# A Fourier mixer followed by a SoLU layer: an entry's first steps begin two steps later, output weights converted without ScalarE, five weight buffers, nine idle products ahead of the step back

## Chip, cores, metric

One core of a Trainium2 chip. The metric is the device time of one execution in microseconds (us), the median of several; lower is better.

## The reference

```python
# mixing: x (8, 3136, 256), filt_r / filt_i (1569, 256)
X = np.fft.rfft(x, axis=1)
Y = X * (filt_r + 1j * filt_i)[None]
y = np.fft.irfft(Y, n=3136, axis=1).astype(np.float32)
# SoLU layer on the 25088 rows of y: w_in (256, 1024), w_out (1024, 256), g_ln (1024)
h = y.reshape(-1, 256) @ w_in
s = h * softmax(h)
ln = (s - mean(s)) / sqrt(var(s) + 1e-6) * g_ln
out = ln @ w_out
```

The weights `w_in` and `w_out` come in 64 bits and are converted to 32 on the core.

## The kernel before

The eight batch entries go one by one through four kinds of work: **first steps** (a short Fourier matrix on rows of x), a **spectrum** (second Fourier step, filter, inverse), and **steps back** (matmuls with `wi_t`, line 353, giving rows of y). Entry 0 does all of this in an *opening* before the main loop. The main loop has 205 *steps* of one block of 128 tokens; each does the SoLU layer of a block and, between its matmuls, pieces of the later entries. `PLAN` says in which step each piece falls: first steps, spectrum units, steps back. "Third entry" is `PLAN[2]`.

```python
PLAN = [
    None,
    ([0, 0, 0, 0, 1, 1, 1, 1], [4, 5, 6, 7, 8, 10, 12], [16, 17, 18, 19, 20, 20, 21, 22]),
    (range(1, 17, 2), range(18, 32, 2), [34, 36, 38, 40, 42, 43, 44, 46]),
    ([17, 23, 25, 27, 29, 31, 33, 35], range(38, 52, 2), range(54, 70, 2)),
    # ... entries 4 to 7
```

Both first steps and steps back read a tile of rows, taken in turn from four buffers. The step in which a row tile is fetched follows from the plan:

```python
    row_loads.sort(key=lambda load: load[0])          # by the step t that uses it
    for n, (t, latest, earliest, load) in enumerate(row_loads):
        at = max(t - 3, earliest, min(row_loads[n - 4][0] + 1, latest) if n >= 4 else -1)
        if at < 0:
            load()
        else:
            loads[at].append(load)                     # issued at the end of step `at`
```

So a tile goes out three steps ahead if it can, but not before the step after the use of the tile four places earlier in the list (`latest` and `earliest` bound this). Loads for the steps back are issued by GpSimd, those of first steps from the third entry on by SyncE.

The end of the opening (`convert` turns one of eight weight pieces to 32 bits; `back` is one step back; its argument is the copy on ScalarE that takes the result out of PSUM; an idle product is a matmul whose result nobody reads, there to keep TensorE busy):

```python
        for i in range(units):
            # ... spectrum of entry 0
            elif i in (1, 3, 4):
                begin({1: 2, 3: 3, 4: 4}[i])           # fetch a weight piece
        idle_row(7, "idler")                           # seven idle products on TensorE
        # ... fetch the rows of the step back, of entry 1, store the filter table (SyncE)
        rest = {2: convert(2)}
        rest.pop(2)()
        begin(5)
        rest[3] = convert(3)
        for ch in range(pieces):
            if ch in (0, 2, 4, 6):
                j = 3 + ch // 2
                rest.pop(j)()                          # ScalarE and GpSimd part of weight j
                if j < 5:
                    begin(j + 3)
                rest[j + 1] = convert(j + 1)           # VectorE part of the next
                if j == 3:
                    weight_sums(w_in_sb)
            for cb in range(KD):
                back(0, ch, cb, nc.scalar.copy)
        rest.pop(7)()
```

## Time and profile before

| | before |
|---|---|
| median, range (first chip, 4 runs) | 1689.76 us, 1688.36 to 1693.68 |
| span of the profiled run, clock | 1694.6 us, 0.981 |
| TensorE busy | 94% |
| VectorE, GpSimd, ScalarE busy | 74%, 67%, 55% |

The clock is the mean share of full speed granted to TensorE; the text calls TensorE cold where it is 0.50 and warm where it is 1.00. The lines that carry the argument are in the prediction.

### The profile page before, as it was taken

How to read it: one execution, taken by the hardware profiler on the slowest of the kernel's cores; microseconds unless marked ns; L12 is line 12 of the kernel's file. 1: busy time of each engine (PE TensorE's matmuls, PEld its weight loads, DVE VectorE, ACT ScalarE, POOL GpSimd, SP SyncE). 2: the span in 40 equal slices, each digit the busy share in tenths (PEclk: the TensorE clock that was granted, in tenths of full speed). 3: DMA queues.
4: the chain of work that ended last, by engine and by line, in shares of the span. 5: the costliest groups of instructions: out<-in, count | busy, mean ns of one | idle time of the engine just before them, and what ended most of it. 6: DMA issues, size and time to landing. Idle time of an engine off the chain costs nothing.

```text
span 1694.6 us, 31047 instructions
## 1 busy us (share of the span) xinstructions
PE 1600.7 (94%) x10008; PEld 1098.7 (65%) x10008; DVE 1259.3 (74%) x2619; ACT 940.0 (55%) x1734; POOL 1131.5 (67%) x1272
## 2 busy tenths in 40 slices
PE   5786899999999999999999999999999999999996
PEld 1362356766766677667766676666776777777776
DVE  1684786788777878787778878787778767777772
ACT  2153456655655565566565665656555666655551
POOL 4463787568756866787568865688556766676664
PEclk8987999999999999999999999999999999999999
DMA  9884767887788768866787658766786455444443
GB/s 262 242 280 151 233 196 195 220 225 196 186 231 237 190 164 228 242 174 167 195 233 212 179 151 226 214 188 170 187 211 176 116 129 123 101 110 102 110 110 94
DMA packets 375957, 311.72 MB, mean 184 GB/s; under 512 B 61514, under 2 KB 341571, under 8 KB 375795
## 3 DMA queue, kind: packets, MB, share of 16 engines
q1 hardware_dynamic: 306260, 169.81, 38.6%
q0 software_dynamic: 32640, 101.65, 20.3%
q10 hardware_dynamic: 36896, 38.28, 8.0%
q8 instruction: 81, 1.33, 0.3%
q14 instruction: 80, 0.66, 0.1%
HBM read 124.83 MB, written 81.50 MB: 122 GB/s over the span
## 4 chain that ended last, share of the span: by engine, by line
PE 62%; DMA 18%; DVE 9%; SPq 3%; POOL 3%; issue 3%; ACT 2%; ACTq 0%; DVEq 0%; POOLq 0%
PE m L682 25%; PE o L794 25%; DMA solu_t<-turn 7%; PE py L353 5%; DMA out_dram<-ot 3%; DMA x<-in_x_dram 2%; SPq L752 2%; PE pa L260 2%; PE pb L292 2%; PE pc L292 2%; DVE h L730 2%; DVE turn L740 1%; DMA t<-d 1%; DVE diff L245 1%; DVE h L706 1%
## 5 line engine op out<-in xcount | busy, mean ns | idle before, releaser
L732 ACT ACTIVATE e<-h,nmu 128x1024 f32<-128x1024 f32 x196 | 225.3, 1150 | 363.4 <-DVE h L730 361.7
L794 PEld LDWEIGHTS o<-w_out_sb,solu_t 128*128 128x128 f32 x3136 | 381.0, 192 | 56.7 <-issue 39.7
L794 PE MATMUL o<-w_out_sb,solu_t 128*128 128x128 f32 x3136 | 401.4, 276 | 8.1 <-DVE rsum L725 4.9
L682 PE MATMUL m<-w_in_sb,s 128*128 128x512 f32 x784 | 400.8, 603 | 2.1 <-ACT h L692 1.9
L794 PEld LDWEIGHTS o<-w_out_sb,u 128*128 128x128 f32 x2352 | 305.6, 192 | 147.2 <-issue 111.6
L660 POOL TENSOR_TENSOR u<-solu_t 128x512 f32<-128x512 f32 x98 | 143.5, 1464 | 305.3 <-DMA solu_t<-turn 190.0
L682 PE MATMUL m<-w_in_sb,y 128*128 128x512 f32 x588 | 315.8, 621 | 25.2 <-DVE nmax L706 22.6
L794 PE MATMUL o<-w_out_sb,u 128*128 128x128 f32 x2352 | 313.2, 276 | 6.9 <-ACT ot L806 5.2
L730 DVE SCALAR_TENSOR_TENSOR h<-e,rsum,h 128x1024 f32<-128x1024 f32 x196 | 286.9, 1464 | 6.9
L813 DVE SCALAR_TENSOR_TENSOR ot<-o,rs_t,ot 128x128 f32<-128x128 f32 x294 | 102.6, 349 | 211.8 <-ACT ot L806 175.0
L692 ACT COPY h<-m 128x512 f32<-128x512 f32 x294 | 173.7, 591 | 127.3 <-PE m L682 117.7
L740 DVE STREAM_TRANSPOSE turn<-h 128x1024 f32<-128x1024 f32 x196 | 242.3, 1236 | 0.8
L714 ACT ACTIVATE e<-h,nmax 128x1024 f32<-128x1024 f32 x196 | 226.2, 1154 | 0.0
L660 POOL TENSOR_TENSOR u<-solu_t,u 128x512 f32<-128x512 f32 x98 | 143.1, 1460 | 87.5 <-PE o L794 83.3
L706 DVE CUSTOM_DVE_ANT_0 h<-m,h 128x512 f32<-128x512 f32 x196 | 133.2, 679 | 76.8 <-ACT h L692 51.3
L682 PEld LDWEIGHTS m<-w_in_sb,y 128*128 128x128 f32 x588 | 96.0, 193 | 134.4 <-DVE nmax L706 76.0
L353 PEld LDWEIGHTS py<-wi_t,t 100*128 100x128 f32 x1024 | 136.8, 198 | 57.2 <-issue 42.0
L356 ACT COPY y<-py 128x392 f32<-128x392 f32 x128 | 109.1, 854 | 103.3 <-PE py L353 101.8
L682 PEld LDWEIGHTS m<-w_in_sb,s 128*128 128x128 f32 x784 | 124.3, 191 | 62.8 <-issue 46.1
L660 POOL TENSOR_TENSOR solu_t<-solu_t,solu_t 128x512 f32<-128x512 f32 x98 | 152.6, 1557 | 7.7
L660 POOL TENSOR_TENSOR u<-u,solu_t 128x512 f32<-128x512 f32 x98 | 140.5, 1433 | 0.7
L353 PE MATMUL py<-wi_t,t 100*128 100x98 f32 x1024 | 136.0, 279 | 4.7 <-ACT y L356 3.5
(106 smaller groups left out, 1979.5 us busy)
## 6 DMA issues: line engine op xcount, KB each, us to landing
solu_t<-turn SPq DMA_DIRECT2D x784, 128.0 KB
out_dram<-ot SPq DMA_DIRECT2D x196, 128.0 KB
t<-d POOLq DMA_DIRECT2D x56, 400.0 KB, 5.0
d<-x POOLq DMA_DIRECT2D x100, 200.0 KB, 4.9
f<-f_dram POOLq DMA_DIRECT2D x39, 512.0 KB, 6.7
d<-g POOLq DMA_DIRECT2D x39, 512.0 KB, 5.0
t<-d ACTq DMA_DIRECT2D x36, 512.0 KB
x<-in_x_dram SPq DMA_DIRECT2D x112, 98.0 KB
```

The source lines that it names most:

```text
L353: nc.tensor.matmul(out=psv[:, i:2 * NCH - i:2 * NCH - 1 - 2 * i, :], lhsT=t4s[e, ch][:, i, cb * P:cb * P + P], rhs=wi_t, start=True, stop= ...
L356: evac(out=y[:, cb, t0:t0 + S].rearrange("p (r m j) -> p m j r", m=N2 // NCH, j=NCH)[:, ch:last + 1 - ch:last - 2 * ch], in_=psv.rearrange ...
L660: nc.gpsimd.tensor_tensor(out=out, in0=in0, in1=in1, op=op)
L682: nc.tensor.matmul(out=ms[j, bank], lhsT=lhsT, rhs=w_in_sb[:, w, :], start=m in (1, 2, 7), stop=True, skip_group_check=True)
L692: nc.scalar.copy(out=h_half(k, i), in_=ms[j, 0])
L706: nc.vector.tensor_tensor_reduce(out=h_half(k, i), in0=ms[j, bank], in1=h_half(*kept), scale=1.0, scalar=sofar, op0=ALU.add, op1=ALU.min, ...
L714: nc.scalar.activation(out=e, in_=hs[k], func=AFT.Exp, bias=nmaxs.pop(k)[:, 1:2], scale=-1.0, accum_out=esum)
L730: nc.vector.scalar_tensor_tensor(out=solu, in0=e, scalar=rsum, in1=solu, op0=ALU.mult, op1=ALU.mult, accum_out=nmu)
L732: nc.scalar.activation(out=e, in_=solu, func=AFT.Square, bias=nmu, scale=-float(DFF), accum_out=variances[g][:, i:i + 1])
L740: nc.vector.transpose(out=turns[g][:, :, i, :], in_=solus.pop(k).rearrange("p (f j) -> p f j", j=32))
L794: nc.tensor.matmul(out=pos[p, bank], lhsT=lhs[:, f, :], rhs=w[:, f, :], start=f == 0 and m in (1, 2, 7), stop=True, skip_group_check=True)
L813: nc.vector.scalar_tensor_tensor(out=ot, in0=pos[p, bank], scalar=rs, in1=out_half(p, *kept)[0], op0=ALU.mult, op1=ALU.add)
```

## The change

The intent is to start the third entry's first steps when their rows have arrived (step 3, not 1), and to free the step back of entry 0 from the weight conversions between which it was threaded.

```diff
-    (range(1, 17, 2), range(18, 32, 2), [34, 36, 38, 40, 42, 43, 44, 46]),
-    ([17, 23, 25, 27, 29, 31, 33, 35], range(38, 52, 2), range(54, 70, 2)),
+    (range(3, 19, 2), range(20, 34, 2), [36, 38, 39, 40, 42, 43, 44, 46]),
+    ([19, 23, 25, 27, 29, 31, 33, 35], range(38, 52, 2), range(54, 70, 2)),
...
-        wpool = pool("wp", 3, stack=st)
+        wpool = pool("wp", 5, stack=st)
... (load_float64, for the output weights)
+                ts(out=power, in0=power, scalar1=255.0, scalar2=2.0 ** 23, op0=ALU.min, op1=ALU.mult)
...
-            def finish():
-                nc.scalar.mul(rest, lo, 2.0 ** -44)
-                nc.gpsimd.tensor_tensor(out=rest, in0=rest, in1=power.bitcast(FP32), op=ALU.mult)
-                nc.gpsimd.tensor_tensor(out=dst, in0=dst, in1=rest, op=ALU.add)
+            if share:                                  # input weights: as before
+                nc.scalar.mul(rest, lo, 2.0 ** -44)
+                nc.gpsimd.tensor_tensor(out=rest, in0=rest, in1=power.bitcast(FP32), op=ALU.mult)
+            else:                                      # output weights: VectorE
+                stt(out=rest, in0=lo, scalar=2.0 ** -44, in1=power.bitcast(FP32), op0=ALU.mult,
+                    op1=ALU.mult)
+            nc.gpsimd.tensor_tensor(out=dst, in0=dst, in1=rest, op=ALU.add)
...
-            elif i in (1, 3, 4):
-                begin({1: 2, 3: 3, 4: 4}[i])
-        idle_row(7, "idler")
+            elif i != 2:
+                begin({1: 2, 3: 3, 4: 4, 5: 5, 6: 6}[i])
+        idle_row(9, "idler")
...
-        (conversions threaded through the step back, as shown above)
+        convert(2)
+        begin(7)
+        convert(3)
+        convert(4)
+        weight_sums(w_in_sb)
+        for j in (5, 6, 7):
+            convert(j)
+        for ch in range(pieces):
             for cb in range(KD):
                 back(0, ch, cb, nc.scalar.copy)
```

More of the change, by code (lines that the diff above doesn't have):

```diff
@@ L372, in load_words, with load_float64 @@
             return raw
-        def load_float64(dst, raw, negate=False):
+        def load_float64(dst, raw, negate, share):
             lo, hi = raw[:, :, 0], raw[:, :, 1]
@@ L385, in load_float64 @@
             ts(out=power, in0=power, scalar1=896.0, scalar2=0.0, op0=ALU.subtract, op1=ALU.max)
-            ts(out=power, in0=power, scalar1=255.0, scalar2=None, op0=ALU.min)
-            ts(out=power, in0=power, scalar1=23, scalar2=-2 ** 31 if negate else 0,
-               op0=ALU.logical_shift_left, op1=ALU.bitwise_or)
+            if negate:
+                ts(out=power, in0=power, scalar1=255.0, scalar2=None, op0=ALU.min)
+                ts(out=power, in0=power, scalar1=23, scalar2=-2 ** 31, op0=ALU.logical_shift_left,
+                   op1=ALU.bitwise_or)
+            else:
+                ts(out=power, in0=power, scalar1=255.0, scalar2=2.0 ** 23, op0=ALU.min, op1=ALU.mult)
             stt(out=power, in0=hi, scalar=-2 ** 31, in1=power, op0=ALU.bitwise_and,
@@ L393, in load_float64 @@
             nc.vector.tensor_tensor(out=frac, in0=frac, in1=power, op=ALU.bitwise_or)
-            def finish():
+            if share:
                 nc.scalar.mul(rest, lo, 2.0 ** -44)
                 nc.gpsimd.tensor_tensor(out=rest, in0=rest, in1=power.bitcast(FP32), op=ALU.mult)
-                nc.gpsimd.tensor_tensor(out=dst, in0=dst, in1=rest, op=ALU.add)
-            return finish
+            else:
+                stt(out=rest, in0=lo, scalar=2.0 ** -44, in1=power.bitcast(FP32), op0=ALU.mult,
+                    op1=ALU.mult)
+            nc.gpsimd.tensor_tensor(out=dst, in0=dst, in1=rest, op=ALU.add)
         filters, tables = {}, {}
@@ L496, in convert @@
         def convert(j):
-            return load_float64(weights[j][0], raws.pop(j), negate=j < 4)
+            load_float64(weights[j][0], raws.pop(j), negate=j < 4, share=j < 4)
         for j in range(2):
-            convert(j)()
+            convert(j)
         def start(i):
@@ L545 @@
                 in_=f[0:rows, at:at + n].rearrange("p i k c -> p i (k c)"))
-        rest = {2: convert(2)}
-        rest.pop(2)()
-        begin(5)
-        rest[3] = convert(3)
-        for ch in range(pieces):
-            if ch in (0, 2, 4, 6):
-                j = 3 + ch // 2
-                rest.pop(j)()
-                if j < 5:
-                    begin(j + 3)
-                rest[j + 1] = convert(j + 1)
-                if j == 3:
-                    weight_sums(w_in_sb)
+        convert(2)
[4 more added lines that the diff above has]
+        for j in (5, 6, 7):
+            convert(j)
+        for ch in range(pieces):
             for cb in range(KD):
                 back(0, ch, cb, nc.scalar.copy)
-        rest.pop(7)()
     ps_b = [pool(f"ps_b{u}", 1, PSUM) for u in range(2)]
```

## The prediction

> **What bounds the kernel now.** I read the page's slices first, then who waited for whom, stretch by stretch, then the engines in order of time. The tenths of busy time over 40 slices (42.4 us each):
>
> ```profile
> PE   5786899999999999999999999999999999999996
> PEclk8987999999999999999999999999999999999999
> ```
>
> TensorE fills its slices from the sixth on (about 212 us), so the steady steps are bound by its work, which the change does not alter. What can be won is idle or slow TensorE time in the first four or five slices. The windows of that part show where it is:
>
> ```profile
> core 0: us, PE busy (x) PEld busy (x) DVE busy (x) ACT busy (x) POOL busy (x), PEclk, DMA share, GB/s
> ...
> 96.00:100.00 4.00, 1.53 (x15) 1.37 (x13) 3.86 (x8) 1.49 (x3) 0.99 (x2) 0.83 1.03 285
> 100.00:104.00 4.00, 4.00 (x19) 4.00 (x20) 3.93 (x6) 1.71 (x3) 2.30 (x2) 0.50 0.58 185
> ...
> 132.00:136.00 4.00, 0.00 (x0) 0.00 (x0) 0.00 (x0) 0.00 (x0) 0.00 (x0) 0.59 0.30 101
> 136.00:140.00 4.00, 1.32 (x2) 0.79 (x3) 2.06 (x5) 0.00 (x0) 1.91 (x3) 0.50 0.05 16
> ```
>
> Two holes, each followed by a stretch at half the clock. The order of time gives what ended them. First hole (matmuls of the step back, line 353, in the opening):
>
> ```profile
> 88.31 6.17 PE L353 MATMUL py<-wi_t,t 100*128 100x98 f32 x48 [0.45 <-DMA t<-d]
> 95.48 2.00 PE L353 MATMUL py<-wi_t,t 100*128 100x98 f32 x16 [1.00 <-ACT y L356]
> 99.94 10.56 PE L353 MATMUL py<-wi_t,t 100*128 100x98 f32 x48 [2.47 <-ACT y L356]
> ```
>
> The same 48 matmuls take 6.17 us and then 10.56 us, the second time at clock 0.50. They waited for ScalarE's evacuation, and ScalarE waited inside a weight conversion, for VectorE:
>
> ```profile
> 98.00 0.42 DVE L381 TENSOR_SCALAR raw<-raw 128x512 int32<-128x512 int32 x1
> ...
> 98.51 0.67 ACT L396 ACTIVATE raw<-raw 128x512 f32<-128x512 int32 x1 [3.15 <-DVE raw L381]
> ```
>
> Second hole, in step 1 of the main loop:
>
> ```profile
> 138.68 2.07 PE L682 MATMUL m<-w_in_sb,y 128*128 128x512 f32 x2 [9.87 <-DVE nmax L706]
> ...
> 137.32 0.69 DVE L245 TENSOR_TENSOR diff<-x 113x512 f32<-113x512 f32 x1 [17.53 <-DMA x<-in_x_dram]
> ```
>
> VectorE stands at the difference of the third entry's first piece (line 245), whose rows landed only at 137.3 us; the maximum behind it (line 706) frees the PSUM bank TensorE wants.
>
> **What the Trainium skill says.** (1) "TensorE: Matmul & The Clock Gate", Part 1: an idle window of about 3.4 us halves the array's clock, and a busy window of that length restores it. The trace agrees on going cold (the holes of about 3.4 and 9.9 us) but not on a quick return here: with these 98-column matmuls the clock stayed at 0.50 until about 112 us. (2) "SBUF — State Buffer", section "SBUF: two separate sides": VectorE in a two-port mode, or with two SBUF inputs, and GpSimd hold a shared pair of ports exclusively; the loser is blocked for the whole instruction. The trace agrees: line 383 takes 418 ns at least and 1518 ns at most, the long ones beside GpSimd's adds of 1.34 us. (3) "DMA: Bandwidth & Descriptors", section "Issuing engines are not separate DMA queues": all issuers share 16 engines. DMA share is 1.03 at 96 to 100 us, so transfers begun earlier may delay others.
>
> **The change, part by part.**
>
> *Opening, ScalarE and the step back.* Today the step back runs from 85.83 to about 110.5 us. Its eight pieces of 16 matmuls take 6.17/3 = 2.06 us each when warm; ScalarE's two evacuations per piece take 1.75 us, so TensorE sets the pace. The change keeps ScalarE out of the conversions of the four output weights, and the two input-weight conversions left on it (81.2 and 82.1 us today) come before the step back. Two more idle products, two passes each of 0.43 us, delay its start by 1.7 us to 87.55. Then 8 x 2.06 = 16.5 us, end at 104.0, against 110.5. The last input row lands near 95 us (issues at 91.96 and 92.31), before its turn at 102. So the step back ends 6.5 us sooner.
>
> *But VectorE's chain is next.* Step 0 has its second first-step product wait for line 706, behind all the conversions in VectorE's order: VectorE is at work without a hole from 77.2 to 114.5 us (busy 3.8 to 4.0 of every 4 us). A conversion without contention costs 3.85 us there (0.34 to 0.46 us for each of six one-input operations, 0.61 for each of two others), plus some 1.05 us for each collision with GpSimd. For an output weight the change merges two of the one-input operations (-0.46), adds one scalar_tensor_tensor (+0.61), and leaves one GpSimd operation of two: 4.0 us with one collision instead of two. In order: weight 2 ends at 81.6 and weight 3 at 88.4 as now; weight 4 needs 5.05, to 93.4; weight sums 3.65, to 97.1; weight 5 finds GpSimd idle, 4.0, to 101.1; weights 6 and 7 take 5.05 each, to 111.2. The pair sums of the first two blocks may collide once more, so line 706 starts at 111.2 to 112, against 114.46. Gain 2.5 to 3.3 us, not 6.5. TensorE, done earlier, then waits some 4 us near 108 to 112 and may go cold; two to three microseconds of recovery at half clock would cost 1 to 1.5. I put the opening at **-2 us**.
>
> *Five weight buffers.* These let weights 5 and 6 be fetched after the units at about 76 to 78 us instead of 85.2 and 90.2. Today VectorE never waits for these (it is busy throughout), so this removes no wait by itself; it allows the plain order of conversions ahead of the step back.
>
> *Third entry from step 3 on.* Its first difference leaves step 1. The 9.87 us wait goes. TensorE's clock no longer falls there: of 138.7 to 142.5 us, 3.8 us at half clock, half comes back, 1.9 us. A wait of 0.73 us on ScalarE's copies of that piece goes too. Its matmuls (eight, 1.8 us) only move to step 17 and its neighbours, where TensorE is full, so they give nothing. Sum **-12.5 us**. Is the row there for step 3? Its difference was at 159.2; the gains above, and 1.8 us of matmuls out of step 1, bring it to about 140. The rows landed at 137.3 today with a second row's transfers behind the same filter stores (SyncE waited 11.1 us for those), and one row less is asked for now. So probably yes, by a few microseconds.
>
> *Later steps.* The third entry's spectrum moves from steps 18 to 30 to steps 20 to 32 and its steps back from 34 to 39. TensorE is at 89 to 94% between 350 and 398 us, so filling there may return a microsecond, or crowd steps 39 and 40. I count nothing.
>
> Sum: 2 + 12.5 = 14.5, rounded to 14 for small waits that come back. 1690.2 - 14 = **1676 us**.
>
> **The rivals.**
> - *The wait moves to step 3.* The row's load goes out at the end of step 0, still behind 3.1 MB of filter stores. For it: DMA share is 0.9 to 1.05 from 112 to 128 us. Against: today's landing is already ahead of the new need. If it lands 5 us late, the time is 1681.
> - *VectorE's chain does not shorten*, because earlier weight transfers hold up the inputs of the step back, or because the new operation collides with GpSimd as often as before. For it: DMA share is near 1 from 84 to 100 us. Against: it is 0.67 at 80 to 84. The opening would then give 0 to +2 us: 1678 to 1680.
> - *The opening gives all of the 6.5 us* and its cold stretch, if TensorE has enough to do before line 706 or VectorE runs freer than I count. Against: no hole in VectorE today. It would make 1670 to 1672.
> - *Later steps take the gain back*: two steps' delay crowds the steps back at 39 and 40, or moves a wait of the second entry's spectrum (3.02 us at 199.7). For 1684 to 1687 most of the 12.5 us would have to be lost; against it, TensorE's steady slices are at 9 and no large wait stands there.
>
> **Range and chances.** The removed wait is the sure part (about 10 us). Opening -6 to +2 and later steps -3 to +5 give 1667 to 1685. Two per cent is 34 us; all idle and cold time that the change touches sums to about 25 (9.9 + 1.9 + 3.5 + 4.4 in the step back + some waits), so faster by over 2% has 3%, slower 1%, within 2% the remaining 96%.
>
> **What would show it.** Right: no wait of 9 us or so of TensorE on line 706 in step 1; the 128 matmuls of the step back in one run of some 16.5 us at clock 1.00, ending near 104; VectorE's conversions still without holes, line 706 first starting at 111 to 112; a TensorE wait of a few us just before it. Wrong: line 245 waiting for its rows in step 3, a step back that waits for its inputs, conversions that end after 114 us, or a step after 16 longer by what was gained.

## More of the kernel before

The profiled execution of before is not a typical one: it took 1696.4 us, 6.6 us more than the median. Waits read from it can be larger than usual.

## The result

| | before | changed |
|---|---|---|
| median, range (4 runs each) | 1689.76 us, 1688.36 to 1693.68 | 1708.24 us, 1704.95 to 1709.57 |
| ratio, 95% interval | | 1.0103, 1.0079 to 1.0126 |
| span of the profiled run, clock | 1694.6 us, 0.981 | 1707.8 us, 0.973 |

A ratio here is the mean time of one kernel's fast runs over that of the other's of the same rounds, so it is not quite the ratio of the medians. All outputs are right. The forecast was 14 us faster and 1667 to 1685 us; it is 18 us **slower** by the medians. By the rule of this record, under which a difference below 2% counts as none, both are "the same"; the interval shows that the loss is real.

To find where, I took from each trace the start of one instruction that occurs once in every step, ScalarE's square of a block (line 732 before, line 730 after), and subtracted. Negative means that the changed kernel is ahead:

| step | 2 | 18 | 20 | 21 | 24 | 34 | 50 | 120 | 182 | 197 | end |
|---|---|---|---|---|---|---|---|---|---|---|---|
| changed minus before, us | -11.4 | -10.3 | -4.0 | +3.1 | +4.4 | +8.0 | +8.3 | +7.4 | +7.3 | +10.3 | +13.2 |

The gain was there at step 2, and it was lost in two places: nearly 14 us between steps 18 and 22, and some 4 to 5 us by step 50. Another 6 us after step 182 belong to this execution alone (see e11). The last column is the difference of the two spans. It is smaller than the 18 us of the medians because the profiled execution of before was 6.6 us over its median. Run e4 below, the same kernel up to step 18, is 5.0 us ahead of it at step 2, so the first columns flatter the change; what is lost from one column to the next does not depend on that.

The page's slices of the changed kernel show the first loss in the eighth slice, where TensorE and its clock dip:

```profile
PE   5898899899999999999999999999999999999996
PEclk8968999899999999999999999999999999999998
```

The changed kernel's order of time for TensorE names what it waited for, in the opening and in steps 20 and 21:

```profile
88.85 26.32 PE L353 MATMUL py<-wi_t,t 100*128 100x98 f32 x128 [3.27 <-DMA t<-d]
...
302.23 2.00 PE L353 MATMUL py<-wi_t,t 100*128 100x98 f32 x8 [3.85 <-DMA t<-d]
...
318.73 2.00 PE L353 MATMUL py<-wi_t,t 100*128 100x98 f32 x8 [4.96 <-DMA t<-d]
```

The first line is the whole step back of entry 0: after a hole of 3.27 us it takes 26.32 us, not 16.5. The other two are steps back of the second entry in the main loop; each waits for its row tile and then runs at half speed (2.00 us; the eight matmuls before the first of these waits took 1.03). One stretch of both kernels, before first (it has the column names):

```profile
core 0: us, PE busy (x) PEld busy (x) DVE busy (x) ACT busy (x) POOL busy (x), PEclk, DMA share, GB/s
304.00:320.00 16.00, 16.00 (x126) 12.39 (x125) 9.07 (x18) 11.52 (x20) 9.49 (x12) 1.00 0.78 212
```

```profile
304.00:320.00 16.00, 11.04 (x62) 7.50 (x61) 6.33 (x11) 5.98 (x9) 4.87 (x8) 0.71 0.54 123
```

Every engine is emptier there after the change, and so are the transfers: this is a wait and no crowd.

**Why the tiles are late.** Working the load rule through for both plans gives, for the steps back of the second entry (pieces counted from 0):

| tile | used in step | fetched in step, before | fetched in step, changed |
|---|---|---|---|
| step back 4 | 20 | 18 | 18 |
| step back 5 | 20 | 18 | **19** |
| step back 6 | 21 | 19 | **20** |
| step back 7 | 22 | 20 | 20 |

The third entry's last first step now falls in step 17, and the fourth entry's first one in 19 instead of 17. The places in the rotation shift by one, and pieces 5 and 6 inherit buffers that come free a step later. A load put in step 19 is issued by GpSimd at the end of that step, behind what stands in its queue. GpSimd in order of time, before and then changed:

```profile
287.64 1.27 POOL L660 TENSOR_TENSOR u<-solu_t 128x512 f32<-128x512 f32 x1 [6.40 <-DMA solu_t<-turn]
...
290.21 0.60 POOL L167 DMA_DIRECT2D t<-d  x1
...
296.78 0.59 POOL L167 DMA_DIRECT2D t<-d  x1
297.60 0.56 POOL L167 DMA_DIRECT2D t<-d  x1 [0.23 <-issue]
```

```profile
294.77 1.26 POOL L658 TENSOR_TENSOR u<-solu_t 128x512 f32<-128x512 f32 x1 [6.02 <-DMA solu_t<-turn]
...
297.33 0.59 POOL L167 DMA_DIRECT2D t<-d  x1
...
309.52 1.27 POOL L658 TENSOR_TENSOR u<-solu_t,u 128x512 f32<-128x512 f32 x1 [8.47 <-PE o L792]
...
311.50 1.14 POOL L167 DMA_DIRECT2D t<-d  x2
```

GpSimd waits some 6 us in both kernels for the transfer of turned activations. With two steps of lead that delay is hidden. With one step, the load at 297.33 is what TensorE waits for until 302.23. While TensorE stands, its products come late, GpSimd waits 8.47 us for one of them (line 792), and the next load goes out at 311.50 only. The two waits of 3.85 and 4.96 us make 8.8 us of the nearly 14. The rest, some 5 us, fits the clock, which was at 0.50 from 302 to 308 us and from 316 to 322 us: TensorE worked about 10 us at half speed there.

### The profile page after: what moved, and what is told of

Same layout as the page of the kernel before.

```text
span 1707.8 us, 31052 instructions
## 1 busy us (share of the span) xinstructions
PE 1616.9 (95%) x10012; PEld 1113.1 (65%) x10012; DVE 1265.6 (74%) x2619; ACT 937.5 (55%) x1730; POOL 1119.5 (66%) x1268
## 4 chain that ended last, share of the span: by engine, by line
PE 64%; DMA 18%; DVE 7%; issue 3%; SPq 3%; POOL 3%; ACT 2%; ACTq 0%; DVEq 0%; POOLq 0%
PE o L792 25%; PE m L680 25%; DMA solu_t<-turn 7%; PE py L353 6%; DMA de<-de_tbl 3%; PE pa L260 2%; SPq L750 2%; PE pc L292 2%; DVE h L728 2%; PE pb L292 2%; DMA x<-in_x_dram 2%; DMA t<-d 2%; PE pa L217 1%; DVE turn L738 1%; ACT e L712 1%
## 5 line engine op out<-in xcount | busy, mean ns | idle before, releaser
L728 DVE SCALAR_TENSOR_TENSOR h<-e,rsum,h 128x1024 f32<-128x1024 f32 x196 | 296.9, 1515 | 6.9
L353 PEld LDWEIGHTS py<-wi_t,t 100*128 100x128 f32 x1024 | 144.8, 210 | 63.5 <-issue 53.0
L353 PE MATMUL py<-wi_t,t 100*128 100x98 f32 x1024 | 143.6, 291 | 12.1 <-DMA t<-d 12.1
```

The costliest lines, as they stand in the source:

```text
L353: nc.tensor.matmul(out=psv[:, i:2 * NCH - i:2 * NCH - 1 - 2 * i, :], lhsT=t4s[e, ch][:, i, cb * P:cb * P + P], rhs=wi_t, start=True, stop= ...
L728: nc.vector.scalar_tensor_tensor(out=solu, in0=e, scalar=rsum, in1=solu, op0=ALU.mult, op1=ALU.mult, accum_out=nmu)
```

## The experiments

**Theory**: the loss after step 18 comes from the two loads with one step of lead. **Rival**: the new opening shifts the phase of everything and causes it. **Second rival**: steps 16 to 22 have simply too much work now. The first group of four separates these.

### e1_old_plan: the new opening with the plan of before

```diff
-    (range(3, 19, 2), range(20, 34, 2), [36, 38, 39, 40, 42, 43, 44, 46]),
-    ([19, 23, 25, 27, 29, 31, 33, 35], range(38, 52, 2), range(54, 70, 2)),
+    (range(1, 17, 2), range(18, 32, 2), [34, 36, 38, 40, 42, 43, 44, 46]),
+    ([17, 23, 25, 27, 29, 31, 33, 35], range(38, 52, 2), range(54, 70, 2)),
```

> The changed kernel with the plan of before; only the opening is new. Late-loads theory (in steps 20 and 21 two rows of the second entry's step back are now fetched only one step ahead, and TensorE waits for them, 14.6 us lost between steps 19 and 22): with the old plan that loss is gone and the wait of step 1 is back, so 1684 to 1694 us. Rival (the new opening, by its shifted phase, is what causes the later loss): the loss stays, 1698 us or more.

Measured: 1690.88 us, ratio 0.9978 (0.994 to 1.0016). No loss between steps 18 and 22. So the opening does not cause it, and the opening by itself is worth nothing that stands clear of noise.

### e2_plan_only: the new plan with the opening of before

The edit is the first hunk of the change alone.

> The kernel before with only the plan changed. Late-loads theory: step 1's wait of about 10 us goes (about 11 us won), 14.6 us are lost between steps 19 and 22 and some 6 us in steps 30 to 40: 1697 to 1704 us, with PE waits on the row loads near steps 20 and 21. Rival (opening causes the loss): 1676 to 1682 us.

Measured: 1700.16 us (1694.79 to 1703.77), ratio 1.0027 (0.9977 to 1.0077), so the time alone shows nothing; the runs of before were wide in this group. The trace is clearer than the time: ahead by 11.2 us at step 18, behind by 2.5 us at step 22.

### e3_spread_back: the changed kernel, no load with less than two steps

```diff
-    ([0, 0, 0, 0, 1, 1, 1, 1], [4, 5, 6, 7, 8, 10, 12], [16, 17, 18, 19, 20, 20, 21, 22]),
+    ([0, 0, 0, 0, 1, 1, 1, 1], [4, 5, 6, 7, 8, 10, 12], [16, 16, 18, 19, 20, 21, 22, 22]),
```

A fifth row buffer would have been the plainer test; it does not build (2.3 KB per partition short), so the steps back were set where the rule of four gives every tile two steps.

> The changed kernel with the second entry's steps back at 16, 16, 18, 19, 20, 21, 22, 22 in place of 16, 17, 18, 19, 20, 20, 21, 22: by the rule of four row buffers every load then goes out two steps ahead or more, and the work of steps 16 to 22 is the same. Late-loads theory: the 14.6 us between steps 19 and 22 come back, 1691 to 1697 us. Rival (steps 16 to 22 are simply too full of TensorE, VectorE and GpSimd work now): 1703 us or more.

Measured: 1693.38 us, ratio 1.0001 (0.9961 to 1.0042). Between steps 18 and 22 the trace gains 1.2 us in place of losing 13.6, with as many pieces of work in these steps. The second rival falls.

### e4_late_loads: the kernel before, with these two loads one step later

```diff
         assert at < t
+        at += n in (16, 17)
```

> The kernel before with nothing changed but two row loads (the second entry's step back, pieces 5 and 6) issued one step later, as the new plan has them. Late-loads theory: PE waits for these rows in steps 20 and 21 and the time rises by 10 to 16 us, to 1700 to 1706 us. Rival (crowding): within 3 us of 1690.

Measured: 1706.27 us, ratio 1.0070 (1.0029 to 1.0111). The kernel before, with nothing else changed, loses 14.0 us between steps 18 and 22, by the same two waits:

```profile
309.44 2.00 PE L353 MATMUL py<-wi_t,t 100*128 100x98 f32 x8 [4.47 <-DMA t<-d]
...
325.53 1.70 PE L353 MATMUL py<-wi_t,t 100*128 100x98 f32 x8 [4.68 <-DMA t<-d]
```

Taking the cause away (e1, e3) and putting it in alone (e4) agree. All the marks, as the change of the difference to the profile of before, in us:

| run | at step 2 | steps 18 to 22 | steps 24 to 50 |
|---|---|---|---|
| changed | -11.4 | +13.6 | +4.0 |
| e11 changed, again | -5.0 | +12.5 | +6.0 |
| e2 new plan only | -10.1 | +13.7 | +5.0 |
| e4 old plan, two late loads | -5.0 | +14.0 | -0.2 |
| e1 new opening only | -5.1 | +0.2 | +0.7 |
| e7 new opening, 17 idle, old plan | -3.5 | 0.0 | +0.5 |
| e3 changed, spread | -9.4 | -1.2 | +5.4 |
| e5 changed, spread, 17 idle | -17.2 | -1.2 | +6.8 |
| e6 changed, spread, weights later | -15.5 | -1.2 | +5.6 |
| e9 changed, spread, tuned | -16.4 | -1.2 | +7.1 |
| e10 new plan, spread, old opening | -15.5 | -0.3 | +3.3 |
| e12 e10 with another step 37 | -14.7 | -0.6 | +5.8 |

Read with care: e4 has the opening of before and is 5 us ahead of before at step 2. One execution's opening differs from another's by that much; TensorE's wait in step 1, for rows on their way, was 9.87 us in before and 3.49 us in e4. The other two columns are much steadier.

The second group asks what became of the opening, and of the gain in step 1.

### e5_spread_idle17: e3 with 17 idle products

```diff
-        idle_row(9, "idler")
+        idle_row(17, "idler")
```

> e3 (changed kernel, steps back spread) with 17 idle products ahead of the step back instead of 9, so that TensorE does not stand still for the 3 to 4 us until the first row of the step back has landed. Cold-hole theory (that one hole halves the clock, and the step back's 98-column matmuls then keep it halved for all of its 26 us): the step back takes 16.5 to 18 us at clock 1.00, although it starts 2 to 4 us later; it ends 6 to 8 us sooner, and the time is 5 to 8 us under e3: 1685 to 1689 us. Rival (these matmuls fall to half clock by themselves, hole or not): clock 0.50 again in the step back, 1692 us or more.

Measured: 1688.26 us, ratio 0.9979 (0.9948 to 1.0011); e3 was at 1.0001, so some 0.2% gained, inside the noise of the times. In the trace it is plain. The step back of e3, then that of e5:

```profile
90.81 26.58 PE L353 MATMUL py<-wi_t,t 100*128 100x98 f32 x128 [3.65 <-DMA t<-d]
```

```profile
93.32 16.52 PE L353 MATMUL py<-wi_t,t 100*128 100x98 f32 x128
```

It starts 2.5 us later and ends 7.6 us sooner. The same matmuls ran at full speed, so it was the hole that made them slow.

### e6_spread_late_weights: e3 with weights 5 and 6 fetched later

```diff
-            elif i != 2:
-                begin({1: 2, 3: 3, 4: 4, 5: 5, 6: 6}[i])
+            elif i in (1, 3, 4):
+                begin({1: 2, 3: 3, 4: 4}[i])
...
         convert(2)
+        begin(5)
+        begin(6)
         begin(7)
```

> e3 with weights 5 and 6 fetched after the conversion of weight 2 (with weight 7) in place of right after the opening's units; nine idle products. Transfer theory (those 1 MB of weights stand in front of the last stores and the first rows of the step back, which therefore land 2 to 3 us later than in the kernel before): the hole ahead of the step back shrinks under 1 us, the step back takes 16.5 to 18 us warm, 1685 to 1689 us. Rival (the first row is late for another reason): the hole of 3 to 4 us and the cold step back of 26 us stay, 1691 to 1696 us.

Measured: 1687.42 us, ratio 0.9972 (0.9947 to 0.9998). The hole ahead of the step back is gone with nine idle products:

```profile
87.64 10.26 PE L353 MATMUL py<-wi_t,t 100*128 100x98 f32 x80
98.26 2.00 PE L353 MATMUL py<-wi_t,t 100*128 100x98 f32 x16 [0.36 <-DMA t<-d]
101.56 7.02 PE L353 MATMUL py<-wi_t,t 100*128 100x98 f32 x32 [1.29 <-DMA t<-d]
```

But the step back took 20.93 us and not 16.5 to 18: after 96 warm matmuls a wait of 1.29 us was enough, and the last 32 ran at clock 0.50. So the forecast of this run was right in the hole and in the time, and missed the length of the step back.

SyncE issues the step back's first row when the opening's last stores have landed; from the start of the first idle product to that issue it takes:

| weights 5 and 6 fetched | runs | us |
|---|---|---|
| right after the opening's units | changed, e11, e3, e5, e8 6.5, e7 6.6, e1 6.2 | 6.2 to 6.6 |
| weight 5 there, weight 6 later | e9 4.5 | 4.5 |
| later | before 1.9, e2 1.7, e4 1.7, e10 2.3, e12 1.7, e6 2.0 | 1.7 to 2.3 |

In the changed kernel and in e6 this reads:

```profile
77.59 7.99 PE L492 MATMUL idler<-f,de 128*128 128x512 f32 x18
84.09 0.33 SPq L172 DMA_DIRECT2D t<-d  x1
```

```profile
79.82 7.99 PE L492 MATMUL idler<-f,de 128*128 128x512 f32 x18
81.84 0.33 SPq L172 DMA_DIRECT2D t<-d  x1
```

So the early weight transfers, 1 MB of them, hold up the stores that the step back waits for, by over 4 us, and one of the two by about half of that. That is what opened the hole. Fetched later they are under way together with the later rows; that the two waits inside the step back of e6 (0.36 and 1.29 us) come from that is likely and not shown.

### e7_old_idle17: the new opening with 17 idle products, the old plan

> The new opening with 17 idle products and the plan of before. If the opening is won back (step back warm), the main loop starts 6 to 8 us sooner than in e1, but step 1 then waits for the third entry's first rows, whose transfers stand behind the filter stores: 3 to 8 us of it are lost there, 1684 to 1691 us. With no such wait, 1683 us.

Measured: 1698.34 us (1694.13 to 1702.84), ratio 1.0045 (1.0014 to 1.0076). My range was missed by 7 us; the profiled execution is the fastest of the four. The step back took 16.52 us here too, but the plan of before then loses it in step 1:

```profile
135.39 2.07 PE L680 MATMUL m<-w_in_sb,y 128*128 128x512 f32 x2 [8.51 <-DVE nmax L704]
```

VectorE stood for the third entry's rows until 134.03 us. Against e5, which differs in the plan only, it is 13.7 us behind at step 2.

### e8_old_idle17_filters_late: e7, filter stores by ScalarE's queue after the step back

> e7 with the four stores of the filter table issued by ScalarE's queue after the step back, so that the third entry's first rows no longer stand behind them in SyncE's queue. If that queue order is what makes step 1 wait, its wait of several us is gone or under 2 us, and the time is 3 to 7 us under e7: 1679 to 1685 us. Rival (the 16 engines are simply full then): no difference from e7.

Measured: 1691.51 us, ratio 0.9995 (0.9972 to 1.0018). My range was missed. The rows for the first difference landed at 137.47 us, no sooner than in e7, and TensorE now waited 4.30 and 2.47 us for rows of the second entry. But this edit does not test the order in SyncE's queue cleanly. SyncE still waited for the filter stores to land, 9.8 us of it among its loads for the second entry, and issued the third entry's loads from 122.28 us on (from 115.76 in e7). Nor were the 16 DMA engines simply full: their share was 0.46 from 128 to 132 us in e7, while VectorE stood. What held these rows stays open, and so does the lower median against e7 (the spans are 1691.7 and 1692.3 us).

### e9_spread_tuned and e10_plan_spread: versions meant to beat both

e9 is e3 with 12 idle products, weight 5 early, weight 6 after the conversion of weight 3, weight 7 after that of 4. e10 is the kernel **before** with the new plan and the spread steps back, the opening left alone.

> A version meant to beat both: the changed kernel with spread steps back (e3), 12 idle products, weight 5 fetched early as in the change, weight 6 after the conversion of weight 3 and weight 7 after that of weight 4. If e5 and e6 read right, TensorE stands still nowhere ahead of the step back or in it for more than 1 us, the step back is warm (16.5 to 18 us), and the time is 1 to 3 us under e5 and e6: 1682 to 1687 us, some 0.3 to 0.5% under the kernel before. If the weights now come too late, VectorE waits for them and it is 1688 us or more.

> The kernel before, its opening untouched, with the new plan and the spread steps back. This is the first-step move alone without the late loads. From the marks of e5 and e7 at step 2 and at step 50, the move wins what step 1's wait costs in that run (5 to 12 us) and gives back 5 us in steps 30 to 50: 1683 to 1692 us, ratio 0.995 to 1.00. If the late loads were not the whole loss of e2: 1695 us or more.

Measured: e9 1688.49 us, ratio 0.9987 (0.9956 to 1.0018), a miss, though its step back ran without a hole in 16.52 us. VectorE became the limit: TensorE waited 2.60 us for line 705 (the maximum of step 0), which started at 111.13 us, and its next six matmuls took 4.52 us, where the same six took 2.88 us in the kernel before. e10 1683.60 us, ratio **0.9951** (0.993 to 0.9972): the best version so far, 25 us under the changed kernel, and clear of noise against before.

### e11_after_again: the changed kernel once more

> The changed kernel once more, beside the others on one chip. Late-loads theory: two waits of TensorE on the rows of the step back in steps 20 and 21 again, 13 to 15 us between steps 18 and 22, 5 to 6 us more by step 50; 1702 to 1710 us. The cold tail after step 190 of the first profile (3 us) may or may not be there; if it is not, it was a matter of that execution.

Measured: 1709.72 us, ratio 1.0108 (1.0082 to 1.0134). Both waits are back (3.16 and 4.99 us). Its trace loses no more after step 182 (9.9 us behind before there, 9.5 at the end). That of the first profile did, from 7.3 to 13.2, with TensorE at half clock once more from 1670 us; those 6 us belong to that execution.

### e12_plan_spread37: e10 with the step back of step 39 in step 37

```diff
-    (range(3, 19, 2), range(20, 34, 2), [36, 38, 39, 40, 42, 43, 44, 46]),
+    (range(3, 19, 2), range(20, 34, 2), [36, 37, 38, 40, 42, 43, 44, 46]),
```

> e10 with the third entry's second piece of the step back in step 37 in place of 39. In the runs with the new plan 3 to 7 us are given back between steps 24 and 50, two of them at steps 39 and 40, where a step back now falls on a step with first steps and the fourth entry's spectrum. If the place of that piece is what costs them: 1680 to 1683 us and 1 to 3 us less given back by step 50 than in e10. If not, the same as e10 within 2 us, and what is given back is the spectrum unit that moved from step 18 to steps 30 to 33.

Measured: 1683.26 us, ratio 0.9947 (0.9933 to 0.9961), the same as e10. It still gives back 5.8 us between steps 24 and 50, so the place of that piece is not what costs them. All nine runs with the new plan give back 3.3 to 7.1 us there; those with the old one change by -0.6 (e8, not in the table) to +0.7. The marks narrow it down: from step 28 to 34 all nine lose 4.2 to 6.7 us, the old plan 0.2 to 1.1. What differs there is the spectrum unit that came from step 18. From the mark of step 30 to that of step 31, in e7 (old plan; the small last unit) and in e5 (new plan; a whole unit):

```profile
399.76:408.78 9.02, 8.86 (x57) 5.83 (x56) 8.48 (x18) 3.23 (x7) 8.39 (x9) 1.00 0.67 183
```

```profile
384.21:395.30 11.09, 9.02 (x62) 6.36 (x64) 10.26 (x18) 3.22 (x6) 8.40 (x11) 1.00 0.77 209
```

TensorE's work hardly differs (8.86 and 9.02 us), but VectorE is busy 10.26 of 11.09 us and TensorE idles 2.07. After the mark of step 18 the same unit stood beside steps back that filled TensorE (in e7, busy for the whole 9.53 us), and taking it out there returned only 2 to 3 us from step 17 to 22 (e3, e5, e10). This fits the numbers; no run moved that unit alone, so it is not shown.

## Why the prediction was wrong, step by step

- **Step 1 (-12.5 us): right in mechanism; its size depends on the opening and on the execution.** The wait on line 706 is gone, and the rows were there for step 3. With a fast opening on both sides (e5 against e7) the move is worth 13.7 us at step 2. With the cold opening of the change as built it is worth between nothing and 6 us (e11, e3 and changed are at -5.0, -9.4 and -11.4, e1 at -5.1). In e1 VectorE waited 3.81 us for these rows, until 129.58 us, and TensorE did not stand on the maximum in step 1 at all. So the two gains of the sum could not simply be added. Also, the waits came from an execution of 1696.4 us and were taken from a median of 1690.2; the wait of 9.87 us was 3.49 us in e4, with the same opening.
- **"Then 8 x 2.06 = 16.5 us, end at 104.0": wrong.** The count was right for a warm array (16.52 us in e5, e7, e9), but it was not warm. The step back took 26.3 us and ended near 115. The failing assumption is in the five weight buffers: "this removes no wait by itself" was true, but it added one. The rival "earlier weight transfers hold up the inputs of the step back" named the cause, though not the effect (VectorE's chain did shorten). I set it aside because the DMA share was 0.67 at 80 to 84 us, but that was measured without the 1 MB of early transfers.
- **VectorE's chain: right in size, no longer the limit.** From the end of weight 2 to that of weight 7 it took 29.9 us (29.6 forecast). It began 2 us earlier than before, so conversions ended at 109.5 us (111.2 forecast), but line 704 (706 before) first ran at 118.31, behind the cold step back. In e9, where the step back was warm, the same line started at 111.13 us, as forecast (111.2 to 112). The rule that the prediction took from "SBUF — State Buffer", section "SBUF: two separate sides", fits: with one GpSimd operation of two taken out of an output weight's conversion, one of its two long VectorE operations went (line 383 at 1.52 us stays, line 396 is at 0.69 us where line 393 took 1.67). So the opening's -2 us came to about nothing: e1 is at 0.9978, with 1 inside its interval. The sum of opening and step 1 was -11.4 us at step 2, against -14.5 forecast; that it comes near is in part luck, since some 5 us of it are the slow execution of before (e11, the same kernel, has -5.0).
- **"Later steps: I count nothing": this is the step that failed.** It was put at 0 and cost 13.6 us between steps 18 and 22, with waits of TensorE of 3.85 and 4.96 us on two row tiles fetched one step ahead and not two, and 4 us more by step 50. It turned the gain into a loss. I had worked the rule for row loads only for the first row of the third entry. The rival "later steps take the gain back" named crowding in steps 39 and 40 and a wait of the second entry's spectrum; the mechanism was another one, a rotation of four buffers in which two tiles lost a step of lead. "No large wait stands there" was read from the profile of before, which can't show a wait that the new plan makes.
- **A misread line.** "Holes of about 3.4 and 9.9 us": no hole of 3.4 us is in the step back of before. The lines show 1.00 us, 2.00 us of work, and 2.47 us, after which the clock was at 0.50. So a shorter hole was enough than the prediction says.

What stays open: the exact cause of the 3 to 7 us in steps 24 to 50, what sets the landing of the third entry's first rows, and why e9, with a clean step back, is not faster than e10 (it is 0.9 us ahead at step 2 and loses 3.8 us more in steps 24 to 50).

## What to carry to other kernels

When a plan moves a piece of work, recompute every load step that follows from the buffer rotation, not only those of the piece that moved: a tile with one step of lead can be held up by whatever stands ahead of its load in the issuing engine's queue. Beginning a transfer earlier can cost time even if nobody waits for that transfer; ask which store or load now comes behind it. Where TensorE would stand ahead of narrow matmuls (3.3 to 4.4 us here), some idle products can be cheaper than the slow stretch that follows: in e5 they brought the end of the step back forward by 7.6 us, though the gain in time, 0.2%, is inside the noise. And read a forecast's waits from an execution whose time is near the median.

## What the Trainium skill lacked or had wrong

- "TensorE: Matmul & The Clock Gate", Part 1, has a busy window of about 3.4 us restore the clock. Here the step back's 128 matmuls of 98 columns, with no gap and TensorE busy 4.00 of every 4.00 us, took 26.3, 27.6, 26.6 and 27.4 us (changed, e1, e3, e11) and ran at clock 0.50 for all but the first 1.4 us at most; the clock rose only when the 512-column matmuls of the main loop had begun (0.80 at 116 to 120 us in the changed kernel). The page does not say which matmuls count as busy. Started warm, the same 128 stayed warm for 16.52 us (e5, e7, e9).
- The same part has an idle window of about 3.4 us halve the clock. The holes of 3.3 to 4.4 us ahead of the step back fit that. But within these 98-column matmuls shorter holes did it too: 1.05 us in e4 (clock 1.00 at 90 to 92 us, 0.50 at 94 to 96), 1.29 us in e6 (1.00 at 98 to 100, 0.50 at 102 to 106), 2.47 us in before.
- "DMA: Bandwidth & Descriptors", "Issuing engines are not separate DMA queues", agrees, and gives no size for it. Here 1 MB of weights that GpSimd issued at 74.10 and 75.96 us, not at 85.21 and 90.22, put off the stores of one engine and the load of another behind them by over 4 us (6.2 to 6.6 against 1.7 to 2.3 us, e6).
